# An attention and mixer kernel on one core: the first batch is normalised behind the product with the values, the second batch's x is turned by DMA, a third unit is loaded ahead of the branch

## The chip, the cores and the metric

The kernel runs on one core of a Trainium2 chip. The metric is the device time of one execution in microseconds. The core's engines are TensorE (PE in the profile, PEld for its weight loads), VectorE (DVE), ScalarE (ACT), GpSimd (POOL) and SyncE (SP), which issues nearly all DMA transfers.

## What is computed

Attention for 4 batches of 8 heads, 768 positions and head size 64, then a token mixer and a channel mixer, all in float32:

```python
def _attn_ref(q, k, v, n_global, n_local) -> np.ndarray:
    ...
    scores = scale * np.matmul(q, k.transpose(0, 1, 3, 2))
    ...
    keep = is_global | is_local
    ...
    scores = scores + bias[None, :, :, :]
    scores = np.where(keep, scores, -1000000000.0)
    scores = scores - np.max(scores, axis=-1, keepdims=True)
    a = np.exp(scores)
    a = a / (np.sum(a, axis=-1, keepdims=True) + 1e-09)
    return np.matmul(a, v).astype(np.float32)

def _moe_ref(x, w_tok1, w_tok2, w_ch1, w_ch2):
    xt = x.transpose(0, 2, 1)
    h = np.maximum(xt @ w_tok1, 0.0) @ w_tok2
    u = x + h.transpose(0, 2, 1)
    h2 = np.maximum(u @ w_ch1, 0.0) @ w_ch2
    return (u + h2).astype(np.float32)
```

Kept are 8 global columns and the 96 positions up to and with a query's own. Between the two, x is the attention's result with heads side by side: 768 positions by 512 channels per batch.

## The kernel before, in words

**Units.** A unit is two heads of one batch and 256 positions. There are 12 units per batch (`PER`), 48 in all. Because only near and global positions are kept, a unit's scores are two blocks of 128 query rows per head (the first positions, j = 0: 128 and 256 columns; later ones: 256 and 256). The two heads of a unit sit in the two halves of TensorE's rows or columns.

**A unit's steps** (`pair`, line 433): load; scale the queries (`q`, tile qs); scores (`S`, tile sp); maxima with the bias added on VectorE (`max`); exponentials with their sums on ScalarE (`exp`, tile pp or p; the statistics are in tile st); sums plus 1e-9 (`sum`) and inverses (`inv`); the scaling of the exponentials by the inverses (`norm`, line 486), always on GpSimd, one instruction per head and cut; the transposes (`T`, tile tp) and their copies back (`back`) or, from unit 20 on (`FAR`), the same by DMA through tile r; the product with the values (`V`, line 526, tile op), which gives x already transposed, channels by positions; and the copy of it to x on ScalarE (`put`, line 543). Units below 15 (`WIDE`) keep their exponentials in one wide tile pp.

**A batch's mixers.** `tokens` (line 592) needs x with positions in the partitions. The first batch turns x on TensorE by half batches (`nat_half`). The second batch (b < `NEAR` = 2) turns it on TensorE too (`nat`, line 602: six calls of four 128x128 transposes into tile xtp). The third and fourth have VectorE split x into 16-bit halves (`xs`, tile xr), eight DMA transposes on SP's queue (`xt`, tile xn), and a step that puts the halves together (`xw`). Then come high and low parts (ph, pl), products with the first token weights (`J`, tile pj), and with the second (`U`, tile pu). `channel` (line 778) is dense matmul work for the first three batches (tiles hp and acc), `blocks` (line 858) the same for the last in a form with fewer products; there the results are gathered in banks ga (512 columns for each of four channel blocks c) and ge (256 columns, one bank shared by blocks c and c + 1), added to x on VectorE (`total`) and stored.

**What sets the order.** `Plan` (line 117) is a list scheduler in Python that runs when the program is built. Every step has an engine (or a choice of engines, by cost), a cost, what it comes after, what it takes and gives (tiles, PSUM banks), and a rank. The planner steps through time and gives each free engine the ready step of least rank; a change between forms of matmul costs it 0.1 or 0.2. The ranks come from a table packed in text (`RANKS`, line 1117, read by `ranks`, line 1163, in eighths). Each engine then runs its instructions in that order and waits by semaphores.

**The start.** `Early` (line 72) stands ahead of a branch on the inputs `n_global` and `n_local`, whose words every engine first loads into registers (`program`, line 1346). It clears a tile, issues the DMAs for the queries and keys of units 0 and 1 (columns 128 to 640 of their tiles; the rest is issued behind the branch), builds positions and distances on GpSimd, and runs `WARM` = 7 matmuls on zeros:

```python
        for i in range(2):
            sp.dma_start(out=self.slots[i][:, 128:640], in_=pk[i, :, 128:640])
...
            for i in range(WARM):
                pe.matmul(out=wp, lhsT=warm[:, :P], rhs=warm, start=i == 0, stop=i == WARM - 1)
```

Units 2 to 11 are loaded whole behind the branch into tiles named unit; later units go through a ring of four tiles (`RING`), named e like the two early ones.

Of the kernel before, what the change touches and what calls it, by code (L numbers as in the profile page):

```python
# [9 lines left out]
F32 = mybir.dt.float32  # L10
# [5 lines left out]
BF16 = mybir.dt.bfloat16  # L16
AF = mybir.ActivationFunctionType
ALU = mybir.AluOpType
# [5 lines left out]
C = H * D  # L24
# [14 lines left out]
NEAR = 2  # L39
FIRST = 0  # L40
WARM = 7
# [30 lines left out]
class Early:  # L72


    def __init__(self, tc, pool, pk, nb):
# [3 lines left out]
        self.slots = [pool.tile([P, 1024], F32, tag=f"e{i}", name=f"e{i}") for i in range(3)]  # L79
# [5 lines left out]
        warm = t[:, 576:832].bitcast(BF16)  # L85
        dve.memset(warm, 0.0)
# [5 lines left out]
        for i in range(2):  # L92
            sp.dma_start(out=self.slots[i][:, 128:640], in_=pk[i, :, 128:640])
# [16 lines left out]

        with tc.tile_pool(name="warm", bufs=1, space=PSUM) as ps:
            wp = ps.tile([P, 512], F32, name="warm")
            for i in range(WARM):
                pe.matmul(out=wp, lhsT=warm[:, :P], rhs=warm, start=i == 0, stop=i == WARM - 1)


class Plan:
# [21 lines left out]
    def record(self):  # L139
# [21 lines left out]
        held_port, marks, sharing, slow = 0.0, [], None, 0.0  # L161
# [88 lines left out]
class Fast:  # L250
# [3 lines left out]
    def __init__(self, ctx, tc, early, pk, nb, w1, w2, wc1, wc2, out):  # L254
# [16 lines left out]
        self.ring = early.slots + [const.tile([P, 1024], F32, tag=f"r{i}", name=f"e{i}") for i in range(RING - 3)]  # L271
# [130 lines left out]
    def load(self, v, first=False):  # L402

        b, n, j = where(v)
        if v < 2:
            t = self.early.slots[v]
            k0, z = 640, 896
        else:
            t = self.wt.tile([P, 1024], F32, tag="w", name="unit") if b == 0 else self.ring[(v - PER) % RING]
            k0, z = (128, 896) if j == 0 else (0, 1024)  # L410
        if not first:
            self.sp.dma_start(out=t[:, k0:z], in_=self.pk[v, :, k0:z])
            if v < 2:
                return
# [3 lines left out]
    def scale(self, v, engine):  # L418

        n = where(v)[1]  # L420
        if v < 2:
            self.load(v, True)
# [10 lines left out]
    def pair(self, v):  # L433
# [5 lines left out]
        far = v >= FAR  # L439

# [35 lines left out]
        def sums():  # L476
            st = g["st"]
            if FIRST <= v < PER:
                pool.tensor_scalar(out=st[:, 8:12], in0=st[:, 4:8], scalar1=EPS, scalar2=0.0, op0=ALU.add, op1=ALU.add)
            else:  # L480
                dve.tensor_scalar(out=st[:, 8:12], in0=st[:, 4:8], scalar1=EPS, scalar2=None, op0=ALU.add)
# [44 lines left out]
        def values():  # L526
# [9 lines left out]

            blocks = ((0, 0, 256, 128), (1, 128, 128, 384), (2, 0, 128, 0))[:2 if j == 0 else 3]
# [12 lines left out]
        if v < 2:  # L550
            add(f"load{v}", "sp", 0.5, lambda: self.load(v), [], rank("load", v), lag=2.6)
        else:
            add(f"load{v}", "sp", (1.4 if j == 0 else 1.85) if v < PER else 0.6, lambda: self.load(v),
                [f"V{v - RING}"] if v >= PER + RING else [f"V{v - PER}"] if v in (PER, PER + 1) else [], rank("load", v),
                ["w"] if v < PER else [], lag=None if v < PER else 3.5)
        if v:
            add(f"q{v}", dict(dve=0.3, act=0.4, pool=0.48) if b == 0 else dict(pool=0.48), 0, lambda e: self.scale(v, e),
                [f"load{v}"] if v > 1 else [], r - 8, ["q"])
# [9 lines left out]
        add(f"sum{v}", *(("pool", 0.32) if FIRST <= v < PER else ("dve", 0.1)), sums, [f"exp{v}0", f"exp{v}1"], r - 12)  # L568
        add(f"inv{v}", "dve", 0.1, inverses, [f"sum{v}"], r - 12)
        for e in range(2):  # L570
            add(f"norm{v}{e}", dict(pool=0.95 if j else 0.83), 0, lambda en, e=e: norm(e, en), [f"inv{v}"], r, parts=2)
        if not far:
            add(f"T{v}", "pe", 0.88 if j else 0.66, transposes, [f"norm{v}0", f"norm{v}1"], r - 5,
# [4 lines left out]
            late, give = "back", wp + (["w"] if 1 < v < PER else [])  # L578
# [279 lines left out]
    def blocks(self, b):  # L858
# [173 lines left out]
        for c in range(4):  # L1032
            n = f"{b}_{f}_{c}"
            add(f"G{b}_{f - 1}_{c}", "pe", 1.04, lambda c=c: second(f - 1, c),
                [f"hl{b}{p}0{m}" for m in range(2)] + [f"low{5 + 2 * f}"] + [f"G{b}_{f}_{c - 1}e" if c else f"G{b}_{f - 2}_3"], k + 3 * c,
                (), ["hid", "hid"] if c == 3 else [])
            add(f"G{n}a", "pe", 0.7, lambda c=c: second(f, c, (0,)), [f"hl{b}{p}1{m}" for m in range(2)] + [f"low{7 + 2 * f}", f"G{b}_{f - 1}_{c}"],
                k + 3 * c + 1)
            add(f"G{n}e", "pe", 0.35, lambda c=c: second(f, c, (1,)), [f"G{n}a"], k + 3 * c + 2, (), ["hid", "hid"] if c == 3 else [])
            for m, x, cost, give in ((0, "a", 0.75, [("ga", b, c)]), (1, "e", 0.35, [("ge", b, c // 2)] if c % 2 else [])):  # L1040
                add(f"out{b}{c}{m}", "dve", cost, lambda c=c, m=m: total(c, m), [f"G{n}{x}"] + ([f"out{b}{c}0"] if m else []), r - 60, (), give)
                add(f"store{b}{c}{m}", "sp", 0.5, lambda c=c, m=m: store(c, m), [f"out{b}{c}{m}"], r - 60, lag=1.6)
# [37 lines left out]
BUSY = dict(dve=1.2, act=0.4, pool=3.0, sp=0.4)  # L1080


def rank(kind, *at):
# [34 lines left out]
    'c-jq>hhG#2;>D-;wllMpU0{JA)`-|n#2C8~xmY6_u_Tf+UPP=!&w^M2L8BOqX!K`@QDZD<L_Hz4Soy_H5yV(%A}GQxyF0tHGv|Ns-sgSad)t-KZ?5SP!'  # L1118
    'Ca&TT;VOz+|(cb!RT3}Q(umKj@)&}O5K88{AG~Le8vO-Cprm;MK&vCt}%=T*>werZOawD@t*<)KqWM*mJmOKuYytPdU=!b74@?#6`mf*&~P=!ejfNIe1'
    '{o8-Bc+4dFU)Mha90zBVzpX!<KR-L@C=}cIYdqI#adg;Bc^+O$}b~%#%zsPus!iOaT}kT);%=67f5k;2VIMse9s=xK4q5I*<9#U~~8o=8y!1ZzH!u60;'  # L1120
    '-va9v$+1U^_{z^&L{aHGZq^Su*wKQ!08kxGF}x$e|W=1;y4y&qV^&EOJUK{AN9lb;fhisA_OH}Do+t)C7$1J@7(@8p$$#MY`~*e7xc@fd%tXXx{wSXc-'
    'CL3byI6B=Eiy#ai$_K{(>`(QINn|VQwcq8bS@DEkgG7GziP$X%*Bu>{DI)H8R{)X*`0+3A}V~n@#LZ`Y)wII8g|HA$ha54|UnVjVQ6F;g?LB^P7A~xit'
# [288 lines left out]
```

## Time and profile before

| | us |
|---|---|
| median of 3 runs | 609.85 (609.1 to 610.99) |
| the profiled execution | 607.03 |
| its span, first to last instruction | 605.3 |
| TensorE busy | 589.9 (97%) |
| VectorE busy | 388.8 (64%) |
| ScalarE busy | 291.5 (48%) |
| GpSimd busy | 190.2 (31%) |
| DMA queue of SP, share of 16 engines' span | 37.9% |

The profile is of one execution. Busy time is the union of an engine's instructions; a matmul's end is modelled, so neighbours overlap in the rows and their distance is best read from start to start. A row of the timeline merges like instructions that follow one another (x8 is eight of them); what stands in brackets is the idle time ahead of it and what ended it. A float32 product shows as two instructions, a transpose as one. The line L63 is that of a helper that issues nearly everything, so operations are told apart by their tiles.

### The profile page before, as it was taken

The page shows a single profiled execution, that of the slowest core. Times are in us where ns is not written, and L with a number is a line of the kernel's source. Part 1 is how long each engine was busy: PE and PEld are TensorE (multiplying, and loading weights), DVE is VectorE, ACT ScalarE, POOL GpSimd, SP SyncE. Part 2 cuts the span into 40 slices and gives each one's busy share as a digit, 9 for nine tenths or more (in the row PEclk, how much of TensorE's full clock was granted, in tenths as well). Part 3 has the DMA queues.
Part 4 walks back from the last instruction along what each step waited for, and adds up shares of the span by engine and source line. Part 5 has one row for each costly group of instructions (what it writes and reads, how often), then busy time and mean ns, then how long its engine had stood idle before and what let it go on. Part 6 is the DMA issues. An engine that isn't in the chain of part 4 may idle for free. (4 is left out here: it accounts for less than half of the span.)

```text
span 605.3 us, 10574 instructions
## 1 busy us (share of the span) xinstructions
PE 589.9 (97%) x3735; PEld 536.9 (89%) x3735; DVE 388.8 (64%) x1007; ACT 291.5 (48%) x777; POOL 190.2 (31%) x303
## 2 busy tenths in 40 slices
PE   6999999999999999999999999999999999999996
PEld 4677799989989899889999999999889999999995
DVE  4989999896641377556854466656778478854223
ACT  5899979884331236452443224244553244332220
POOL 5788774644320035233321024343241020000000
PEclk9999999999999999999999999999999999999999
DMA  7971291632730012666937001766756000100003
GB/s 257 376 262 46 108 329 53 229 119 62 157 88 26 2 53 52 145 145 149 188 73 172 4 26 40 158 125 150 169 98 110 0 2 17 37 1 1 0 1 109
DMA packets 84172, 62.63 MB, mean 103 GB/s; under 512 B 69776, under 2 KB 74128, under 8 KB 84112
## 3 DMA queue, kind: packets, MB, share of 16 engines
q1 hardware_dynamic: 83968, 61.88, 37.9%
q8 instruction: 31, 0.51, 0.3%
q14 instruction: 29, 0.24, 0.1%
q10 hardware_dynamic: 144, 0.00, 0.0%
HBM read 38.80 MB, written 6.29 MB: 74 GB/s over the span
## 5 line engine op out<-in xcount | busy, mean ns | idle before, releaser
L63 PE MATMUL hp<-uh,wc 128*128 128x384 f32 x576 | 153.9, 337 | 0.0
L63 PE MATMUL acc<-hh,wc 128*128 128x384 f32 x576 | 148.7, 339 | 0.7 <-DVE hl L63 0.7
L63 PEld LDWEIGHTS acc<-hh,wc 128*128 128x128 f32 x576 | 102.8, 188 | 6.0 <-issue 3.8
L63 PEld LDWEIGHTS hp<-uh,wc 128*128 128x128 f32 x576 | 104.5, 188 | 3.6 <-issue 1.9
L63 POOL TENSOR_SCALAR p<-p,st 128x256 f32<-128x256 f32 (+1 forms) x132 | 77.7, 608 | 93.5 <-ACT p L63 49.3
L63 DVE COPY r<-p 128x1024 uint16<-128x1024 uint16 (+1 forms) x96 | 66.9, 717 | 54.4 <-DMA p<-r 33.6
L63 PE MATMUL acc<-hl,wc 128*128 128x384 f32 x288 | 96.7, 336 | 0.2 <-DVE hl L63 0.2
L63 PE MATMUL hp<-ul,wc 128*128 128x384 f32 x288 | 96.3, 334 | 0.0
L63 ACT ACTIVATE hh<-hp 128x384 fp32r<-128x384 f32 x72 | 35.1, 489 | 85.9 <-PE hp L63 58.6
L63 ACT ACTIVATE p<-p,st 128x256 f32<-128x256 f32 (+1 forms) x132 | 63.6, 484 | 14.2 <-DVE st L63 14.2
L63 DVE SCALAR_TENSOR_TENSOR hl<-hp,hh 128x384 fp32r<-128x384 f32 x72 | 39.3, 550 | 41.0 <-ACT hh L63 36.3
L63 PEld LDWEIGHTS acc<-hl,wc 128*128 128x128 f32 x288 | 54.0, 188 | 0.7 <-DVE hl L63 0.7
L63 PEld LDWEIGHTS hp<-ul,wc 128*128 128x128 f32 x288 | 54.1, 188 | 0.1
L63 POOL TENSOR_TENSOR ul<-x,uh 128x384 fp32r<-128x384 f32 x19 | 21.3, 1125 | 97.2 <-ACT uh L63 93.2
L63 POOL TENSOR_SCALAR qs<-e,sc 128x256 f32<-128x256 f32 x36 | 22.1, 617 | 57.3 <-DMA e<-pk 51.8
L63 PE MATMUL sp<-e,qs 64*128 64x256 f32 (+1 forms) x304 | 38.0, 384 | 1.0 <-DVE few L63 0.9
L63 ACT COPY r<-p 128x1024 uint16<-128x1024 uint16 (+1 forms) x16 | 20.8, 1302 | 36.0 <-DMA p<-r 28.5
L63 POOL TENSOR_SCALAR pp<-pp,st 128x256 f32<-128x256 f32 (+1 forms) x60 | 33.1, 569 | 4.5 <-DVE st L63 4.2
L63 PEld LDWEIGHTS sp<-e,qs 64*128 64x128 f32 x304 | 26.4, 194 | 8.6 <-issue 3.6
L63 PE MATMUL ga<-hh,wc 128*128 128x512 f32 x96 | 30.2, 395 | 0.0
L63 ACT ACTIVATE pp<-pp,st 128x256 f32<-128x256 f32 (+1 forms) x60 | 28.5, 481 | 3.0 <-DVE st L63 2.9
L63 PE MATMUL op<-r,e 128*64 128x128 f32 (+1 forms) x304 | 27.6, 318 | 0.7 <-DVE st L63 0.4
(146 smaller groups left out, 1096.8 us busy)
## 6 DMA issues: line engine op xcount, KB each, us to landing
w<-wc SPq DMA_DIRECT2D x24, 512.0 KB, 6.1
e<-pk SPq DMA_DIRECT2D x24, 512.0 KB, 4.3
e<-pk SPq DMA_DIRECT2D x12, 384.0 KB, 3.6
out<-o SPq DMA_DIRECT2D x24, 192.0 KB, 1.9
unit<-pk SPq DMA_DIRECT2D x8, 512.0 KB, 7.9
w<-w SPq DMA_DIRECT2D x6, 512.0 KB, 9.5
out<-x SPq DMA_DIRECT2D x8, 192.0 KB, 1.9
p<-r SPq DMA_TRANSPOSE x56, 3.4
```

The lines of the kernel that those rows point to most:

```text
L63: ins = getattr(self.engine, name)(*args, **kw)
```

## The change

- **Third unit.** The ring's fourth tile is made early. Keys and queries of unit 2 are loaded into it ahead of the branch, as a third DMA on SP; the rest of it follows behind the branch with that of units 0 and 1. Unit 15, which uses this ring tile next, now waits for unit 2's product.
- **Warm matmuls.** Four instead of seven, and behind the register loads, ahead of the branch.
- **First batch (`fold`).** No scaling by the inverses ahead of the transposes, which now wait for the exponentials alone. The product with the values is preceded by four matmuls that write the inverses of each query column, broadcast over 64 rows, to columns 256 to 512 of the same bank. ScalarE copies that part to x (`pi`), VectorE multiplies the product with it (`put`). Sums may go to GpSimd or VectorE.
- **Second batch.** `NEAR` = 1: x is turned like that of the third and fourth.
- **Last products.** In even channel blocks of the last stage the 256-column part (ge) goes ahead of the 512-column part (ga); in odd ones it stays behind.
- **Planner.** It takes the first 3.4 us of TensorE for slow, the engines are free a little later (`BUSY`), and all ranks are replaced by a new table in halves.

The diff, cut to its core (the new table of ranks is left out):

```diff
-NEAR = 2
+NEAR = 1
-WARM = 7
+WARM = 4
...
-        for i in range(2):
-            sp.dma_start(out=self.slots[i][:, 128:640], in_=pk[i, :, 128:640])
+        for i, x, k in ((0, 0, 128), (1, 1, 128), (2, 3, 0)):
+            sp.dma_start(out=self.slots[x][:, k:640], in_=pk[i, :, k:640])
...
+    def warm(self, tc):
         with tc.tile_pool(name="warm", bufs=1, space=PSUM) as ps:
...
-        held_port, marks, sharing, slow = 0.0, [], None, 0.0
+        held_port, marks, sharing, slow = 0.0, [], None, CRAWL
...
-        if v < 2:
-            t = self.early.slots[v]
-            k0, z = 640, 896
+        if v < 3:
+            t = self.early.slots[(0, 1, 3)[v]]
+            k0, z = 640, 896 if v < 2 else 1024
...
+        fold = b == 0
...
+            for i, e in ((i, e) for i in range(2 if fold else 0) for e in range(2)):
+                k = 8 + 2 * e + i
+                self.pe.matmul(out=op[64 * e:64 * e + 64, 256 + P * i:256 + P * i + P], lhsT=g["st"][:, k:k + 1].broadcast_to([P, 64]),
+                               rhs=self.ident, start=True, stop=True)
...
-        def put():
+        def put(step=0):
             for m, o, c, w in (((0, 0, 0, 256),), ((0, 256, 0, 128), (1, 0, 128, 128)), ((1, 128, 0, 256),))[j]:
-                act.copy(out=self.x[b, n, m][:, o:o + w], in_=g["op"][:, c:c + w])
+                x, y = self.x[b, n, m][:, o:o + w], g["op"]
+                if step == 1:
+                    dve.tensor_tensor(out=x, in0=y[:, c:c + w], in1=x, op=ALU.mult)
+                else:
+                    act.copy(out=x, in_=y[:, c + 256 * fold:c + 256 * fold + w])
...
-        for e in range(2):
+        for e in range(0 if fold else 2):
             add(f"norm{v}{e}", dict(pool=0.95 if j else 0.83), 0, lambda en, e=e: norm(e, en), [f"inv{v}"], r, parts=2)
         if not far:
-            add(f"T{v}", "pe", 0.88 if j else 0.66, transposes, [f"norm{v}0", f"norm{v}1"], r - 5,
+            add(f"T{v}", "pe", 0.88 if j else 0.66, transposes, [f"{'exp' if fold else 'norm'}{v}{e}" for e in range(2)], r - 5,
...
-        add(f"V{v}", "pe", 0.86 if j else 0.65, values, ([f"load{v}"] if v < 2 else []) + [f"{late}{x}{e}" for x in twins for e in range(2)] + ([f"V{v - (4 if b else 2)}"] if twins and j else []) or [f"V{v - 1}"],
+        add(f"V{v}", "pe", (0.86 if j else 0.65) + 0.25 * fold, values, ([f"load{v}"] if v < 3 else []) + ([f"inv{v}"] if fold else []) + [f"{late}{x}{e}" for x in twins for e in range(2)] + ([f"V{v - (4 if b else 2)}"] if twins and j else []) or [f"V{v - 1}"],
-        add(f"put{v}", "act", 0.34 if j == 1 else 0.28, put, [f"V{v}"], r - 15, (), [("op", v)])
+        if fold:
+            add(f"pi{v}", "act", 0.34 if j == 1 else 0.28, put, [f"V{v}"], r - 15)
+            add(f"put{v}", "dve", 0.45 if j == 1 else 0.35, lambda: put(1), [f"pi{v}"], r - 15, (), [("op", v)])
+        else:
+            add(f"put{v}", "act", 0.34 if j == 1 else 0.28, put, [f"V{v}"], r - 15, (), [("op", v)])
...
+            order = (("e", 0.35), ("a", 0.7)) if c % 2 == 0 else (("a", 0.7), ("e", 0.35))
+            for i, (x, cost) in enumerate(order):
+                add(f"G{n}{x}", "pe", cost, lambda c=c, x=x: second(f, c, (0 if x == "a" else 1,)),
...
-BUSY = dict(dve=1.2, act=0.4, pool=3.0, sp=0.4)
+BUSY = dict(dve=1.8, act=0.8, pool=3.0, sp=1.0)
...
-    return [x / 8.0 for x in struct.unpack(f"<{len(data) // 2}h", data)]
+    return [x / 2.0 for x in struct.unpack(f"<{len(data) // 2}h", data)]
...
     _, (g_lo, g_hi, l_lo, l_hi) = nc.values_load_multi_w_load_instructions(nb)
+    early.warm(tc)
```

## Rows read from the trace of the kernel before

**Rows 1.** The page: busy times (shares of the span), and TensorE in 40 slices.

```profile
PE 589.9 (97%) x3735; PEld 536.9 (89%) x3735; DVE 388.8 (64%) x1007; ACT 291.5 (48%) x777; POOL 190.2 (31%) x303
PE   6999999999999999999999999999999999999996
```

**Rows 2.** Table by stretches: stretch and length, busy us per engine, PEclk, DMA, GB/s.

```profile
10.86:15.62 4.76, 4.76 (x20) 3.61 (x21) 2.83 (x12) 2.84 (x10) 2.97 (x9) 1.00 1.02 417
15.62:45.00 29.38, 26.94 (x239) 20.79 (x239) 25.87 (x92) 27.19 (x87) 22.60 (x41) 1.00 0.86 316
45.00:81.00 36.00, 34.96 (x281) 28.58 (x281) 33.76 (x96) 35.08 (x105) 30.64 (x45) 1.00 0.31 113
```

**Rows 3.** Timeline of TensorE from the start: start us, length, instructions, idle before.

```profile
1.20 3.17 PE L63 MATMUL warm<-e 128*128 128x512 bf16 x7 [1.20 <-DVE e L63]
5.25 2.93 PE L63 MATMUL sp<-e,qs 64*128 64x128 f32 x16 [0.89 <-DVE few L63]
10.86 2.08 PE L63 MATMUL sp<-unit,qs 64*128 64x256 f32 x8 [2.67 <-DVE qs L63]
12.87 2.82 PE L63 MATMUL tp<-ident,pp 128*128 128x128 f32 x12
15.62 1.42 PE L63 MATMUL sp<-unit,qs 64*128 64x256 f32 x8
16.97 1.52 PE L63 MATMUL op<-pp,e 128*64 128x256 f32 x16
18.43 1.13 PE L63 MATMUL sp<-unit,qs 64*128 64x256 f32 x8
```

**Rows 4.** Timeline: SP's issues for units 0 to 2, and unit 2's scaling.

```profile
0.75 0.89 SPq L63 DMA_DIRECT2D e<-pk  x2
...
4.68 0.81 SPq L63 DMA_DIRECT2D e<-pk  x2
...
5.53 0.43 SPq L63 DMA_DIRECT2D unit<-pk  x1
...
10.45 0.35 DVE L63 TENSOR_SCALAR qs<-unit,sc 128x256 f32<-128x256 f32 x1 [0.82 <-DMA unit<-pk]
```

**Rows 5.** Timeline of TensorE: transposes of the second batch's x, first twelve.

```profile
195.06 1.47 PE L63 MATMUL xtp<-ident,x 128*128 128x128 f32 x12
...
196.29 0.60 PE L63 MATMUL acc<-hh,wc 128*128 128x384 f32 x2
```

**Rows 6.** Groups on GpSimd, 0 to 80 us: busy us, mean ns, idle before.

```profile
L63 POOL TENSOR_SCALAR pp<-pp,st 128x256 f32<-128x256 f32 x46 | 25.9, 575 | 3.8 <-DVE st L63 3.6
...
L63 POOL TENSOR_SCALAR pp<-pp,st 128x128 f32<-128x128 f32 x14 | 7.7, 549 | 0.7 <-DVE st L63 0.6
```

**Rows 7.** Timeline of TensorE: the value products of two later units.

```profile
27.30 1.96 PE L63 MATMUL op<-pp,unit 128*64 128x256 f32 x24
29.18 1.13 PE L63 MATMUL sp<-unit,qs 64*128 64x256 f32 x8
```

**Rows 8.** Groups on VectorE, whole span: the nearest product out of PSUM.

```profile
L63 DVE TENSOR_TENSOR x<-ge,x 128x256 f32<-128x256 f32 x4 | 1.7, 419 | 1.2 <-PE ge L63 1.2
```

**Rows 9.** Tiles xr and xn, later batches: duration ns min/median/max, then landing.

```profile
L63 DVE COPY xr<-x x16: 532/554/1653, 273.5 to 463.9; 128x768 uint16<-128x768 uint16 x16
L63 SPq DMA_TRANSPOSE xn<-xr x16: 1212/1234/1572, 275.0 to 466.7; - x16
...
L63 DVE COPY xw<-xn x8: 741/748/761, 323.8 to 473.8; 128x1024 uint16<-128x1024 uint16 x8
...
DMA to landing us min/median/max: 2.8/3.0/6.2
```

**Rows 10.** Timeline near the end: the weight load that waits for VectorE.

```profile
599.06 0.30 PEld L63 LDWEIGHTS ge<-hh,wc 128*128 128x128 f32 x2 [0.25 <-DVE x L63]
```

**Rows 11.** Timeline: second batch's last copy to x, first token product.

```profile
192.96 0.38 ACT L63 COPY x<-op 128x256 f32<-128x256 f32 x1 [0.54 <-PE op L63]
...
199.36 0.39 PE L63 MATMUL pj<-ph,w1h 128*128 128x512 f32 x1
```

More of the change, by code (lines that the diff above doesn't have):

```diff
@@ L77, in __init__ @@
         pe, dve, act, gps, sp = [InOrder(tc, e) for e in (nc.tensor, nc.vector, nc.scalar, nc.gpsimd, nc.sync)]
-        self.slots = [pool.tile([P, 1024], F32, tag=f"e{i}", name=f"e{i}") for i in range(3)]
+        self.slots = [pool.tile([P, 1024], F32, tag=f"e{i}", name=f"e{i}") for i in range(RING)]
         self.ni = pool.tile([P, 4], I32, tag="ni", name="ni")
@@ L84, in __init__ @@
         t = self.slots[2]
-        warm = t[:, 576:832].bitcast(BF16)
-        dve.memset(warm, 0.0)
+        self.zeros = t[:, 576:832].bitcast(BF16)
+        dve.memset(self.zeros, 0.0)
         self.one = t[:, 832:836]
@@ L113, in __init__ @@
             for i in range(WARM):
-                pe.matmul(out=wp, lhsT=warm[:, :P], rhs=warm, start=i == 0, stop=i == WARM - 1)
+                tc.nc.tensor.matmul(out=wp, lhsT=self.zeros[:, :P], rhs=self.zeros, start=i == 0, stop=i == WARM - 1)
 class Plan:
@@ L269, in __init__ @@
         const = self.const = pool("const", 1)
-        self.ring = early.slots + [const.tile([P, 1024], F32, tag=f"r{i}", name=f"e{i}") for i in range(RING - 3)]
+        self.ring = early.slots
         self.wt = pool("wt", 2 * NF)
@@ L474, in exps, with sums @@
                                bias=g["st"][:, k:k + 1], accum_out=g["st"][:, 4 + k:5 + k])
-        def sums():
+        def sums(engine):
             st = g["st"]
[L478 to L481, printed above, removed]
+            engine.tensor_scalar(out=st[:, 8:12], in0=st[:, 4:8], scalar1=EPS, scalar2=0.0, op0=ALU.add, op1=ALU.add)
         def inverses():
@@ L557, in pair @@
             add(f"q{v}", dict(dve=0.3, act=0.4, pool=0.48) if b == 0 else dict(pool=0.48), 0, lambda e: self.scale(v, e),
[L558 removed]
+                [f"load{v}"] if v > 2 else [], r - 8, ["q"])
         wp = ["w"] if wide else ["p", "p"]
@@ L577, in pair @@
                     r - 10, (), [("tp", v, e)])
-            late, give = "back", wp + (["w"] if 1 < v < PER else [])
+            late, give = "back", wp + (["w"] if 2 < v < PER else [])
         else:
@@ L1034, in blocks @@
             add(f"G{b}_{f - 1}_{c}", "pe", 1.04, lambda c=c: second(f - 1, c),
-                [f"hl{b}{p}0{m}" for m in range(2)] + [f"low{5 + 2 * f}"] + [f"G{b}_{f}_{c - 1}e" if c else f"G{b}_{f - 2}_3"], k + 3 * c,
+                [f"hl{b}{p}0{m}" for m in range(2)] + [f"low{5 + 2 * f}"] + [f"G{b}_{f}_{c - 1}{'ea'[c % 2]}" if c else f"G{b}_{f - 2}_3"], k + 3 * c,
                 (), ["hid", "hid"] if c == 3 else [])
-            add(f"G{n}a", "pe", 0.7, lambda c=c: second(f, c, (0,)), [f"hl{b}{p}1{m}" for m in range(2)] + [f"low{7 + 2 * f}", f"G{b}_{f - 1}_{c}"],
-                k + 3 * c + 1)
-            add(f"G{n}e", "pe", 0.35, lambda c=c: second(f, c, (1,)), [f"G{n}a"], k + 3 * c + 2, (), ["hid", "hid"] if c == 3 else [])
+            order = (("e", 0.35), ("a", 0.7)) if c % 2 == 0 else (("a", 0.7), ("e", 0.35))
+            for i, (x, cost) in enumerate(order):
+                add(f"G{n}{x}", "pe", cost, lambda c=c, x=x: second(f, c, (0 if x == "a" else 1,)),
+                    [f"G{n}{order[0][0]}"] if i else [f"hl{b}{p}1{m}" for m in range(2)] + [f"low{7 + 2 * f}", f"G{b}_{f - 1}_{c}"],
+                    k + 3 * c + 1 + i, (), ["hid", "hid"] if c == 3 and i else [])
             for m, x, cost, give in ((0, "a", 0.75, [("ga", b, c)]), (1, "e", 0.35, [("ge", b, c // 2)] if c % 2 else [])):
-                add(f"out{b}{c}{m}", "dve", cost, lambda c=c, m=m: total(c, m), [f"G{n}{x}"] + ([f"out{b}{c}0"] if m else []), r - 60, (), give)
-                add(f"store{b}{c}{m}", "sp", 0.5, lambda c=c, m=m: store(c, m), [f"out{b}{c}{m}"], r - 60, lag=1.6)
+                add(f"out{b}{c}{m}", "dve", cost, lambda c=c, m=m: total(c, m), [f"G{n}{x}"] + ([f"out{b}{c}{1 - m}"] if m == c % 2 else []), r - 60, (), give)
+                add(f"store{b}{c}{m}", "sp", 0.5, lambda c=c, m=m: store(c, m), [f"out{b}{c}{x}" for x in range(m + 1)], r - 60, lag=1.6)
     def run(self):
```

95 lines of the change are left out of this document (48 added, 47 removed).

## The prediction
> **What bounds the kernel now.** I read the page's shares first. TensorE is busy for 589.9 of 605.3 us and its row of slices reads 9 everywhere except in the first and the last slice [rows 1]. So the bound is TensorE's work plus its few idle stretches, and an edit counts only by the matmul time it adds or takes away, or by an idle or slow stretch of TensorE that it closes. The table by stretches comes next: from 15.62 to 45 us TensorE idles 29.38 - 26.94 = 2.4 us and from 45 to 81 us 1.0 us, together 3.5, while ScalarE works 27.19 of 29.38 and 35.08 of 36, VectorE 25.87 and 33.76, GpSimd 22.60 and 30.64 [rows 2]. In this stage (first batch) all engines are nearly full; after it TensorE alone is. Then TensorE's own timeline from the start. The scores of units 0 and 1 begin at 5.25, unit 2's at 10.86, after 2.67 us of idleness that ended with the scaled queries qs [rows 3]. Why so late: SP issues two loads ahead of the branch (0.75 to 1.64), gets past the branch at 4.68, issues unit 2 only at 5.53, and VectorE, which scales it at 10.45, had waited for that DMA [rows 4].
>
> **The clock at the start.** The granted clock column reads 1.00 from 10.86 to 15.62 [rows 2], but the matmuls say otherwise: the eight instructions of unit 2's scores take 2.08 us at 10.86 and the same eight 1.13 at 18.43, and twelve transposes take 12.87 to 15.62 = 2.75 us [rows 3] where twelve later ones take 195.06 to 196.29 = 1.23 [rows 5]. So until about 15.6 us the array is at the lower of its two levels, 1.2 GHz, and from then at 2.4. Ahead of the rise TensorE had worked without a gap since 10.86; the seven warm matmuls and the first scores, with gaps of 0.89 and 2.67 us between, had not brought it.
>
> **The change part by part.**
>
> *Third unit ahead of the branch.* Unit 2's keys and queries come behind units 0 and 1 on SP's queue, into a slot of their own, so its scores can follow unit 1's at 8.2 us: the 2.67 us go. On SP's queue the third issue costs some 0.4 us (two took 0.89 [rows 4]), so all that SP issues behind the branch, from the first two values halves to unit 3 and the weights, comes 0.4 us later; one values load more (unit 2's) stands there too. Their next user is unit 3's scores, at 15.62 now, which leaves cover; without it those scores would come 0.8 us later. Term: **-2.7**. With no idle stretch in the way the clock should rise earlier. If it rises at the end of unit 2's scores, the twelve transposes save 2.75 - 1.23 = 1.5 us; if also during the first scores, up to some 4 us; if it still rises at 15.6, the 2.67 us won are worked at half speed and 1.3 of them are lost again. I take **-1.5**, between +1.3 and -4, by the transposes, the work that stands right behind.
>
> *Warm matmuls.* Four instead of seven, behind the register loads. Seven take 3.17 us, so four take 1.8 [rows 3]. SP's stretch from its last issue at 1.64 to 4.68 bounds the register loads and branch at 3.0 us [rows 4]. Starting with them, TensorE would be through by about 3.5 and warm until 5.3, and unit 0's scores start at 5.25 anyway, so between 0 and +0.2; I take 0. Cover gone (loads slower), each microsecond is one of delay.
>
> *Normalisation behind the product.* The first batch loses its GpSimd scalings between exponential and transpose. Up to 80 us GpSimd has 46 of 575 ns and 14 of 549 ns on wide tiles [rows 6], four for each of the fifteen units that use such tiles; twelve of these are the first batch, so 48 go, about 27 us. They lie on GpSimd, not on TensorE, so directly they give nothing; but each unit's way from exponential to transpose is 4 x 0.57 = 2.3 us shorter. In their place TensorE gets four matmuls per unit, each a column of inverses broadcast against the identity, 128 columns, one per head and cut. No such matmul is in the trace; the nearest are the value products of the same output shape. Two units with two blocks take 16.97 to 18.43 = 1.46 us, 0.73 each [rows 3], two with three blocks 27.30 to 29.18 = 1.88, 0.94 each [rows 7]: one 128-column block for both heads costs 0.21. Two blocks per unit and twelve units: **+5.0**, all on the path, since TensorE is the bound. The planner's own cost is 0.25 per unit, 3.0 in all; I take the rows, and keep 3.0 as the lower end and, should the broadcast weights load slower, 6.5 as the upper. ScalarE copies as many columns as before. VectorE gets the multiplication, nearest row x<-ge at 0.42 us for 256 columns out of PSUM [rows 8]: some 12 x 0.45 = 5.4 us, against 5.8 us of idleness in rows 2, and GpSimd's freed 27 us can take subtractions and scalings off it. The product now also waits for the inverses, and the output bank is held by two steps instead of one.
>
> *Waits of TensorE from 15.6 to 81.* 3.5 us [rows 2]. The softmax chain is shorter, GpSimd is free, but VectorE has more to do. Between none left (-3.5) and 3 us more, I take half of them gone: **-1.7**. The new table of ranks reorders everything here and shows in no row; these bounds are to hold it.
>
> *Second batch's x turned by DMA.* TensorE loses 24 transposes (six calls of four). Twelve took 1.23 us [rows 5]: **-2.5**. In their place VectorE splits (0.55 us, eight), SP's queue carries eight DMA transposes (1.23 us of issue, 3.0 to land), and VectorE puts halves together (0.75 us, six), as the later batches do [rows 9]; 15 us or so of VectorE and SP in a stretch where TensorE has a channel stage to work on. The casts and subtractions behind stay. Cover gone: rival D.
>
> *Order of the last matmuls.* The last product into ge of an odd column block waits 0.25 us for VectorE's read of the even one, at 599.06 [rows 10] and once more, 4.3 us earlier in the same pattern. With ge first in even blocks the read falls under the 512-column products: **-0.5**, at worst 0. The last block keeps its order, so the end stays.
>
> Sum: -2.7 - 1.5 + 5.0 - 1.7 - 2.5 - 0.5 = **-3.9 us**. The profiled execution took 607.03 us, 605.3 of span and 1.7 around it, and would come to 603.1; it lies 2.8 us below the median of the runs shown, 609.85, which by the same difference gives 605.95, **606.0 us**. What a measurement of this kernel can tell from no change is 0.3%, 1.8 us.
>
> **Rivals.**
>
> *B, VectorE becomes the bound (slower).* Place: 15.6 to 81 us. It works 59.6 of 65.4 us there [rows 2]. If it keeps its share of idleness (it waits on the others in turn) and gets 5.4 us more with nothing taken off, the stage takes 65.4 x 65.0 / 59.6 = 71.3 us, 5.9 more, and the start's gain becomes waits for the multiplied x. Left are +5.9 - 2.5 - 0.5 = +2.9: **612.8**. It decides while GpSimd takes less than about 3 us off VectorE, for each of them gives back 1.1. For it: the shares above. Against: GpSimd freed by 27 us, and the start's work 2.7 us earlier.
>
> *C, the start gives little.* Clock rise unchanged, waits in the stage down by only 1.2: -2.7 + 1.3 + 5.0 - 1.2 - 2.5 - 0.5 = -0.6: **609.3**. This is also what comes out if the change doesn't do what it says, unit 2 landing early but being scaled late. For it: the row that shows the rise tells only what went before it. Against: GpSimd idles early, and can scale.
>
> *D, the turned x comes late.* After the second batch's last copy (192.96, 0.38 us) the first product with the token weights starts at 199.36 [rows 11], 6.0 us later, filled with other matmuls. The way by DMA takes 0.55 + 4 x 1.23 + 3.0 + 0.75 = 9.2 us for a half of four tiles. If nothing fills it, 3.2 us are lost: **609.2**. Against: the first half's tiles are ready sooner, only the second half hangs on the last copy, and TensorE waits nearly nowhere in later batches, which turn x this way. The Trainium skill, VectorE: DVE Perf Modes, "Rules for kernel authors", speaks against this part: a 128x128 transpose belongs on TensorE where the result may go to PSUM, and on the DMA crossbar only otherwise. The rows agree that one transpose is far shorter there, 0.10 against 1.23 us of issue alone. By that rule the sum would be better without this part's -2.5, or it comes to this rival; the rule does not ask which engine is full.
>
> *E, all ends good.* Broadcasts at 3.0, the clock up during the first scores, no waits left: -2.7 - 4.0 + 3.0 - 3.5 - 2.5 - 0.5 = -10.2: **599.7**.
>
> **Chances and numbers.** The forecast 0.55, as TensorE's own terms are read from rows and its start is plainly idle; E 0.10, C 0.17, D 0.05, B 0.13. Faster by over 0.3%: forecast and E, 0.65. Within 0.3%: C and D, 0.22. Slower: B, 0.13. The range runs from 601.0, which leaves out E's far end, to 611.5, which holds C and D and the forecast with costlier broadcasts, and leaves out most of B. The forecast's own range is 603 to 608.
>
> **What would show it.** Unit 2's scores right behind unit 1's at some 8.2 us, and the doubled durations gone before 12 us. 48 (or 96, as float32 instructions come in pairs) new TensorE rows from the statistics and the identity, whose stretch per unit is 0.42 us; 0.25 or less would set that term too high. No first-batch scaling of exponentials on GpSimd. The rows xtp halved, 24 DMA transposes xn instead of 16, no TensorE wait near 200 us. No wait for ge at the end. Idle TensorE between 15 and 81 us under 3.5. Wrong if TensorE's idleness there grows by more than the start gains, above all with VectorE named as the releaser, or if the clock rises no earlier.

## The result, and the profile after

The changed kernel takes **601.31 us** (median of six runs, 600.73 to 602.05), the kernel before on the same chip 609.57 (six runs, 608.05 to 610.99): ratio 0.9865, 95% interval 0.9848 to 0.9882, or **8.3 us less**. The forecast said faster, by 3.9, to 606.0, with its own range from 603 to 608; the result lies 0.3 us inside the lower end of the whole range, 601.0. A second set gave 601.12 against 608.26, ratio 0.9885 (0.986 to 0.9911). The profiled executions differ less, 607.03 and 601.20, because the one of before lies below all six runs above: two more took 609.99 and 608.21.

The page's shares and slices of the changed kernel: TensorE still bounds it, and GpSimd has lost 12.6 us.

```profile
PE 587.3 (98%) x3804; PEld 537.7 (90%) x3804; DVE 392.8 (66%) x1026; ACT 297.3 (50%) x778; POOL 177.6 (30%) x265
PE   7999999999999999999999999999999999999996
```

The table by stretches, to be held against [rows 2]. TensorE's idleness between 15.62 and 81 us falls from 3.5 to 0.9 us; VectorE fills up (28.09 of 29.38), GpSimd empties (12.59 for 22.60).

```profile
10.86:15.62 4.76, 4.76 (x40) 3.60 (x41) 4.76 (x23) 4.30 (x18) 0.94 (x3) 1.00 1.04 412
15.62:45.00 29.38, 28.48 (x286) 23.21 (x284) 28.09 (x98) 28.12 (x89) 12.59 (x17) 1.00 0.92 354
45.00:81.00 36.00, 36.00 (x317) 30.50 (x314) 32.72 (x109) 33.16 (x99) 23.67 (x33) 1.00 0.26 89
```

TensorE's timeline from the start, against [rows 3]. The scores of units 0, 1 and 2 are one row without a pause, but they begin at 6.10, 0.85 us later than before.

```profile
1.20 1.89 PE L115 MATMUL warm<-e 128*128 128x512 bf16 x4 [1.20 <-DVE e L63]
6.10 4.64 PE L63 MATMUL sp<-e,qs 64*128 64x128 f32 x24 [3.02 <-DVE e L63]
10.68 1.26 PE L63 MATMUL tp<-ident,pp 128*128 128x128 f32 x6
11.87 1.14 PE L63 MATMUL sp<-unit,qs 64*128 64x256 f32 x8
12.93 0.88 PE L63 MATMUL tp<-ident,pp 128*128 128x128 f32 x6
...
14.80 0.66 PE L63 MATMUL op<-ident,st 128*64 128x128 f32 x8
15.29 0.82 PE L63 MATMUL op<-pp,e 128*64 128x256 f32 x8
15.94 0.61 PE L63 MATMUL op<-ident,st 128*64 128x128 f32 x8
16.37 0.82 PE L63 MATMUL op<-pp,e 128*64 128x256 f32 x8
```

The broadcasts (op from ident and st) take 0.49 and 0.43 us a unit, start to start. SP's queue, against [rows 4], has a third issue ahead of the branch, and its next one at 5.71 instead of 4.68. The first scaling of queries on VectorE, which waits for its load in both kernels, starts at 4.90 instead of 4.38. With the third load taken out again (below) the scores start at 5.22, so the third load is what makes the start late; through which step all of the 0.85 comes, no row tells.

```profile
0.75 1.36 SPq L63 DMA_DIRECT2D e<-pk  x3
5.71 0.33 SPq L63 DMA_DIRECT2D unit<-pk  x1
```

TensorE's list of waits is short (engine, tile, what it waited for; us in all, times, longest): two at the start, one among the first batch's transposes (at 34.4) and three in the later mixers. Its weight loads, which [rows 10] showed waiting for VectorE ahead of ge, stand without a wait from 586 us on.

```profile
PE sp L63 <- DVE e L63: 3.0, 1, 3.0
PE warm L115 <- DVE e L63: 1.2, 1, 1.2
PE acc L63 <- DVE st L63: 0.9, 2, 0.5
PE tp L63 <- DVE pp L63: 0.8, 1, 0.8
PE hp L63 <- DVE hl L63: 0.2, 1, 0.2
```

The list of before has three entries that lie between 15.62 and 81 us and that are gone here. The first stands at 21.39, and the profile shows nothing that ended it.

```profile
PE sp L63 <- issue: 1.2, 1, 1.2
...
PE op L63 <- ACT pp L63: 1.0, 3, 0.4
...
PE xtp L63 <- ACT x L63: 0.8, 1, 0.8
```

**Two stages.** The first product of the channel stage (tile hp) is a good milestone: in either order the same TensorE work stands ahead of it, but for the broadcasts, three warm-up products fewer and one more unit's scores (1.06 us) in the changed kernel. Read from the timelines:

| kernel | hp starts | from there to TensorE's end | idle in that part |
|---|---|---|---|
| before, three profiles | 80.90, 80.87, 79.98 | 518.78, 521.09, 520.18 | 1.47, 2.67, 1.95 |
| changed, two profiles | 80.12, 79.84 | 513.44, 513.08 | 1.05, 1.04 |

So up to the milestone the change wins 80.58 - 79.98 = 0.6 and 1.06 of work done, 1.7 us; behind it 520.0 - 513.3 = 6.8, of which 1.06 is that work, so 5.7. The forecast had 0.9 and 3.0. These are few profiles, though. Four of the variants below (without the third unit, without the fold, with 7 and with 10 warm-up products) have the changed kernel's work and order behind hp, and there they take 514.15, 515.57, 513.55 and 514.87. The six together have a mean of 514.1, and the 5.7 becomes 4.8.

### The profile page after: what moved, and what is told of

It is laid out like the page before. It is cut to its first block, busy times and chain, and to the rows that moved or that the text cites. A ratio compares the mean times of both kernels' runs of the same rounds, so it can differ in the third digit from the quotient of the medians.

```text
span 599.1 us, 10678 instructions
## 1 busy us (share of the span) xinstructions
PE 587.3 (98%) x3804; PEld 537.7 (90%) x3804; DVE 392.8 (66%) x1026; ACT 297.3 (50%) x778; POOL 177.6 (30%) x265
## 4 chain that ended last, share of the span: by engine, by line
PE 56%; DMA 3%; DVE 2%; issue 0%; ACT 0%; SPq 0%; DVEq 0%
PE acc L63 16%; PE hp L63 13%; PE ga L63 6%; PE X L63 4%; PE op L63 3%; PE pj L63 3%; PE pu L63 3%; PE ge L63 3%; PE sp L63 2%; PE W L63 2%; DMA p<-r 2%; PE Y L63 1%; DMA xn<-xr 1%; DVE r L63 1%; DVE o L63 1%; DVE p L63 0%
## 5 line engine op out<-in xcount | busy, mean ns | idle before, releaser
L63 DVE COPY r<-p 128x1024 uint16<-128x1024 uint16 (+1 forms) x89 | 63.7, 732 | 40.3 <-DMA p<-r 24.9
L63 POOL TENSOR_TENSOR ul<-x,uh 128x384 fp32r<-128x384 f32 x23 | 25.4, 1109 | 94.3 <-ACT uh L63 92.4
L63 ACT COPY r<-p 128x1024 uint16<-128x1024 uint16 (+1 forms) x23 | 29.1, 1285 | 29.1 <-DMA p<-r 17.5
L63 PE MATMUL sp<-e,qs 64*128 64x256 f32 (+1 forms) x312 | 39.3, 389 | 3.0 <-DVE e L63 3.0
L63 PEld LDWEIGHTS sp<-e,qs 64*128 64x128 f32 x312 | 27.8, 197 | 10.9 <-issue 8.4
L63 ACT COPY x<-op 128x256 f32<-128x256 f32 (+1 forms) x64 | 18.9, 322 | 25.6 <-PE op L63 25.4
L63 DVE CUSTOM_DVE_ANT_0 p<-sp,be 128x256 f32<-128x256 f32 x48 | 20.0, 416 | 12.2 <-PE sp L63 10.8
```

The lines of the kernel that those rows point to most:

```text
L63: ins = getattr(self.engine, name)(*args, **kw)
```

## Experiments

All ratios are against the kernel before, run on the same chip in the same set. Differences in us are between medians of a set; where the ratio gives another difference by 0.4 us or more, it stands beside. In each variant but the one of before with more warm-up products, the order is written out as a list, and where a part was taken out or put in, the list was mended. The profile of a variant is one of its executions, and not always a usual one.

**The changed kernel with its order written out**, a second sample of it.

> The changed kernel, with every engine's order of work written out as a list in place of the ranks; the instructions and their order are the changed kernel's own. Account theory and order theory alike: 601.3, within 0.5 of the changed kernel's median, so that the variants beside it can be set against it. If it comes out more than 1 us from that, the variants may only be compared with one another. Its profile is a second execution of the changed kernel: if the start is what makes executions differ, the granted clock should rise at another time than the 11.8 us of the first profile.

601.12 us (600.04 to 601.74), ratio 0.9885 (0.986 to 0.9911). Its profile repeats the first, the scores of units 0 to 2 at the low level again. The variants below are set against 601.12.

**Without the third unit ahead.**

```diff
-        if v < 3:
-            t = self.early.slots[(0, 1, 3)[v]]
...
+        if v < 2:
+            t = self.early.slots[v]
...
```

> The changed kernel and its order, but unit 2 is loaded whole behind the branch. Account theory (what TensorE waits for at the start is lost for good): 2.7 for the wait, 1.4 for the clock's later rise, less 0.85 because the branch is left earlier with two loads ahead of it: 3.2 us slower than the changed kernel. Rival (the start is caught up later, since the units behind it wait for other things): 0 to 1 us slower.

606.63, ratio 0.9978 (0.9962 to 0.9993): 5.5 us above the changed kernel, more than either theory. Its third unit is scored at 12.68, after 4.53 us of waiting for queries that ScalarE scaled only when their load had come, and still at the low level. hp starts at 85.03, 5.1 later: what is lost at the start is not caught up. The rival falls.

```profile
12.68 2.08 PE L63 MATMUL sp<-unit,qs 64*128 64x256 f32 x8 [4.53 <-ACT qs L63]
```

**Without the folded normalisation.**

```diff
-        fold = b == 0
+        fold, FIRST_ = False, b == 0
...
-        for e in range(0 if fold else 2):
+        for e in range(2):
...
```

> The changed kernel with the first batch normalised by GpSimd ahead of its transposes again, no broadcasts on TensorE; over the first 85 us of the plan the order is mended where work would otherwise stand behind a later normalisation, elsewhere it is the changed kernel's. Account theory (the fold costs 5.0 of broadcasts and gives back 2.6 of waits): 2.4 us faster than the changed kernel. Rival (the shorter chain is what lets the early order run without waits, so that it is worth more than its broadcasts): 2 to 7 us slower than the changed kernel, with the loss in waits for normalised p and the probabilities' copies before 81 us.

607.77, ratio 0.9987 (0.9965 to 1.0009): 6.6 us above the changed kernel (6.2 by the ratios) although 5.7 us of broadcasts are gone. The account theory falls, and the time is what the rival said. TensorE's waits in this kernel:

```profile
PE tp L63 <- POOL pp L63: 2.7, 3, 1.9
...
PE op L63 <- DVE pp L63: 1.3, 2, 0.8
```

The transposes wait for GpSimd's normalised p, which the changed kernel does not have to wait for. Only part of the 6.6 us can be read, as this execution (604.95) was 2.8 us under its own median. Its hp starts at 82.31, 2.3 later: TensorE idles 3.8 us more ahead of it, the rows of op are 1.9 and those of the scores 1.8 us longer, the broadcasts' 5.7 are gone. The scores are longer because a unit's eight still take 2.08 us at 14.90, the low level, where the changed kernel has 1.14 at 11.87.

**Without x by DMA.**

```diff
-NEAR = 1
+NEAR = 2
```

> The changed kernel with the second batch's x turned by TensorE again (six groups of four transposes, no DMA transposes of x, no packing and unpacking copies); from 125 to 230 us of the plan the order is mended where it would stall. Account theory: the transposes' 2.5 us of TensorE come back, 2.5 us slower than the changed kernel. Rival D (x turned by DMA comes late and its copies load VectorE): the same or up to 0.7 us faster than the changed kernel.

604.82, ratio 0.9947 (0.993 to 0.9964): 3.7 us above the changed kernel. hp starts at 79.91, so all of it lies behind. Summed by tile over that part, from one group's start to the next, the transposes xtp add 2.5 us and TensorE's idleness 1.1 (2.11 for 1.04), in these waits above all:

```profile
PE hp L63 <- DVE hl L63: 0.7, 1, 0.7
...
PE op L63 <- DVE r L63: 0.5, 1, 0.5
PE op L63 <- ACT p L63: 0.2, 1, 0.2
```

Only the first of them, at 195.6, stands where the turned x is used. The 0.5 is at 294, and TensorE's idleness behind hp is 1.04 to 2.45 us in the six profiles with the changed kernel's work there. Against their mean of 514.1 this kernel's 516.95 is 2.8 longer. So the account theory's 2.5 stands and rival D falls; that the part is worth more than its transposes is not shown, as the two ratios' intervals leave 1.2 to 6.3 us.

**Without the exchange of the last products** (the lines of the diff that make `order` go back).

> The changed kernel with the last products and output sums of the last channel in the order of the kernel before. Account theory: the last sum waits again for the bank of the second products, 0.5 us slower than the changed kernel (601.7). Rival (the output store behind it hides it): the same within 0.2.

602.25, ratio 0.9891 (0.9867 to 0.9914) against 0.9885 for the changed kernel: 0.4 us by the ratios, 1.1 by the medians of two sets on two chips, not told apart from nothing.

**The third unit alone, in the old order.**

```diff
-        for i in range(2):
-            sp.dma_start(out=self.slots[i][:, 128:640], in_=pk[i, :, 128:640])
+        for i, x, k in ((0, 0, 128), (1, 1, 128), (2, 3, 0)):
+            sp.dma_start(out=self.slots[x][:, k:640], in_=pk[i, :, k:640])
...
```

> The kernel before and its order, with the third unit's k and q loaded ahead of the branch; units 2 and 4 change places in the first steps, so that unit 2, not unit 4, is scored third. Account theory: the wait of 2.7 less 0.85 for the later branch, and 1.4 for the clock's earlier rise: 3.2 us faster than before. Rival (given back: the transposes of the first units now wait for normalised p, since the order behind is the old one): 0 to 1 us faster.

611.39, ratio 1.0045 (1.003 to 1.0061), **2.8 us slower** than before. Both theories fall as to the time; of the rival's mechanism there is more than it asked. The timeline shows where the 2.67 us went: into new waits of the transposes for GpSimd. And the low level lasts longer: a unit's scores take 2.08 us at 16.16 and the value products behind them are slow too, where before has the scores at 1.13 from 18.43 and sixteen value products in 1.52 [rows 3].

```profile
5.84 4.55 PE L63 MATMUL sp<-e,qs 64*128 64x128 f32 x24 [1.47 <-DVE e L63]
11.55 1.22 PE L63 MATMUL tp<-ident,pp 128*128 128x128 f32 x6 [1.16 <-POOL pp L63]
14.45 1.78 PE L63 MATMUL tp<-ident,pp 128*128 128x128 f32 x6 [1.68 <-POOL pp L63]
16.16 2.08 PE L63 MATMUL sp<-unit,qs 64*128 64x256 f32 x8
18.17 2.39 PE L63 MATMUL op<-pp,e 128*64 128x256 f32 x12
```

**The folded normalisation alone, in the old order** (the diff's lines in `pair` on fold, norm, pi and put).

> The kernel before and its order, with the first batch normalised behind the product with the values (48 broadcasts more on TensorE, 24 normalisations less on GpSimd, 24 multiplications on VectorE). Account theory: broadcasts 5.0 less the waits for normalised p that go, 2 to 2.6: 2.4 to 3 us slower than before. Rival (the order was made for the long chain, nothing is gained): 5 us slower. Rival (the chain was what held the start): 0 to 1 us slower.

611.98, ratio 1.0047 (1.0028 to 1.0065), 3.4 slower (2.9 by the ratio): nearest to the account theory, under the first rival's 5. In its profile hp starts at 85.63, 5.0 later, for 5.7 of broadcasts: TensorE idles 1.6 us less ahead of it, and its scores take 1.3 more.

**Three parts together, in the old order** (third unit, fold, last products).

> The kernel before and its order with three of the four parts: third unit ahead, normalisation behind the product, last products exchanged; x of the second batch is still turned by TensorE. Account theory: -3.2 + 2.6 - 0.5: 1.1 us faster than before, so that the order and x by DMA hold the remaining 7. Rival (the parts help each other: with the third unit ahead and no normalisation to wait for, the start runs through): 4 to 5 us faster than before.

611.76, ratio 1.007 (1.0044 to 1.0095), 3.2 slower than before (4.3 by the ratio); both theories fall. hp starts at 84.83, although the first scores ran at the high level and the transposes began at 8.33:

```profile
5.95 2.44 PE L63 MATMUL sp<-e,qs 64*128 64x128 f32 x24 [1.62 <-DVE bo L63]
8.33 1.52 PE L63 MATMUL tp<-ident,pp 128*128 128x128 f32 x7
...
12.29 1.13 PE L63 MATMUL sp<-unit,qs 64*128 64x256 f32 x8 [0.97 <-POOL qs L63]
13.36 0.66 PE L63 MATMUL op<-ident,st 128*64 128x128 f32 x8
16.16 0.87 PE L63 MATMUL op<-pp,e 128*64 128x256 f32 x8 [2.14 <-ACT pp L63]
```

The product of unit 0 now stands waiting for ScalarE's copy of the transposed p. Between unit 0's transposes and this product the old order has unit 1's transposes and one unit's scores; the changed order has a second unit's scores there as well, and shows no wait.

**The new order alone**, with none of the four parts.

```diff
-NEAR = 1
+NEAR = 2
...
-        if v < 3:
...
+        if v < 2:
...
-        fold = b == 0
+        fold, FIRST_ = False, b == 0
...
```

> The changed kernel's order of work, from the changed kernel's table, without any of the four parts: unit 2 loaded whole behind the branch, the first batch normalised by GpSimd ahead of the transposes, the second batch's x turned by TensorE, the last products as before; over the first 230 us of the plan the order is mended where work would stall. Theory 'the order is worth something by itself' (the parts lose 3 us in the old order, the order gains 10 with or without them): about 600. Theory 'the order is only good for the parts' (what the three parts cost when each is taken out of the changed kernel adds up, 5.5 + 6.6 + 3.7): 617.

612.8, ratio 1.0071 (1.0046 to 1.0096), 4.4 slower; the second theory is nearer, but nothing adds up. hp starts at 87.11, with two units' scores (2.1 us) more ahead of it than in before, and the start shows the units' scores late again:

```profile
5.22 2.93 PE L63 MATMUL sp<-e,qs 64*128 64x128 f32 x16 [2.13 <-DVE few L63]
9.03 2.08 PE L63 MATMUL sp<-unit,qs 64*128 64x256 f32 x8 [0.88 <-POOL qs L63]
12.84 2.08 PE L63 MATMUL sp<-unit,qs 64*128 64x256 f32 x8 [1.74 <-ACT qs L63]
```

With three parts (all but x by DMA) and the order, this makes a table of four corners, each against before in its own set:

| | without the three parts | with them |
|---|---|---|
| old order | 0 | +3.2 (three parts) |
| new order | +4.4 (order alone) | -3.4 (without x by DMA) |

Parts and order each lose by themselves; together they win 3.4, which is 11.0 us under the sum of the two losses (11.8 by the ratios). The row of the new order also has the four warm-up products in place of seven, whose number is worth nothing measurable below. And what the third unit, the fold and x by DMA cost when each is taken out of the changed kernel adds up to 15.8, twice what the change wins.

**x by DMA alone, in the old order.**

```diff
-NEAR = 2
+NEAR = 1
```

> The kernel before and its order, with the second batch's x turned by DMA instead of by TensorE; the packing copies stand where the attention output that they read comes, the unpacking copies behind the last unit's maxima, and from 188 to 230 us of the plan the order is mended where it would stall. Account theory: 2.5 us of transposes go, 2.5 us faster than before. Rival D (the turned x comes late: the last unit's output is ready shortly before the products with it, and packing, DMA, unpacking and splitting now stand between them): 1 to 5 us slower than before, with waits of the products pj for the copies around 190 to 210 us.

609.71, ratio 1.0012 (0.999 to 1.0033): no difference, so the account theory falls. Rival D does not stand either: there is no wait of pj, and no loss clear of noise. Of the transposes' 2.4 us nothing is left: behind hp TensorE idles 5.20 us, against 1.5 to 2.7 in before, above all at 123.0 and at 213.0:

```profile
PE sp L63 <- POOL qs L63: 1.4, 1, 1.4
...
PE pu L63 <- DVE pl L63: 0.9, 1, 0.9
```

**Warm-up products.** Three runs on the clock at the start.

```diff
-WARM = 4
+WARM = 7
```

> The changed kernel with 7 warm-up products in place of 4, nothing else. Theory of the early clock (the scores of units 0 to 2 run at the low level, 0.19 us a product, as TensorE stood for 3.0 us before them; in the profile of the three parts in the old order, with 7 warm-up products, they took 0.10): the stretch from the first score to the first transpose falls from 4.6 to 2.4 us, and the kernel becomes up to 2.2 us faster. Rival (the exponentials of unit 0 are not there earlier; TensorE waits for them instead): the same within 0.5, with a new wait ahead of the first transposes.

602.57, ratio 0.9898 (0.9873 to 0.9924); hp at 79.31, and no wait ahead of the first transposes. The stretch from the first score to the first transpose fell only from 4.6 to 4.0 us, so this profile decides neither theory; no time was won.

```profile
5.82 4.04 PE L63 MATMUL sp<-e,qs 64*128 64x128 f32 x24 [1.45 <-DVE e L63]
```

And with 10:

> The changed kernel with 10 warm-up products in place of 4, so that TensorE works up to 5.7 us. Theory: the scores of units 0 to 2 take 2.4 in place of 4.6 us, and since nothing waits there the kernel gains 1 to 2 us (600). Rival (the exponentials set the start): tp waits, the first channel's products start within 0.5 us of 79.9, the time is the same within 0.5.

602.93, ratio 0.9902 (0.9886 to 0.9918), so nothing won and at most a little lost; hp at 79.0. The scores of units 0 to 2 now run at the high level, and 2.2 us are won there; the next units' scores then wait for GpSimd's scaled queries, as the rival says of waits, though on another tile:

```profile
5.75 2.44 PE L63 MATMUL sp<-e,qs 64*128 64x128 f32 x24 [0.76 <-DVE e L63]
8.13 1.24 PE L63 MATMUL tp<-ident,pp 128*128 128x128 f32 x6
9.86 1.13 PE L63 MATMUL sp<-unit,qs 64*128 64x256 f32 x8 [0.49 <-POOL qs L63]
10.92 1.19 PE L63 MATMUL tp<-ident,pp 128*128 128x128 f32 x6
13.17 1.14 PE L63 MATMUL sp<-unit,qs 64*128 64x256 f32 x8 [1.06 <-POOL qs L63]
```

The kernel before with 9 in place of 7:

> The kernel before with 9 warm-up products in place of 7, so that TensorE works up to the first scores at 5.25 us. Theory (the clock's rise changes the time and the long pause ahead of the third unit does not bring it down again): the first scores run at the high level, the first channel's products start 2 us earlier, 606.5. Rival (the scores of units 0 and 1 only end earlier and TensorE waits longer for the third unit; what follows is at the low level again, or the waits take the rest): the same within 1 us.

609.48, ratio 1.0007 (0.9982 to 1.0032), hp at 80.41: the first scores ran at the high level (1.73 us for 16), then came 3.24 us of waiting, then the low level again. The rival stands.

**The kernel before, twice more.**

> The kernel before itself. 609.6, within 0.5. Its profile is a second execution. Theory of the early clock (the profiled execution of before, 2.5 us under its own median, was one in which the granted clock happened to rise early): this profile's execution shows the rise later than 15.4 us into the span, and a span nearer 607.5. Rival (the difference is a drift of all stages alike): the rise is at 15.4 again, and the times of the groups differ by a few tenths of a per cent throughout.

> The kernel before a third time, for its profile alone. If the 2.3 us by which the second profile was longer behind 81 us is chance from execution to execution: the first channel's products at 80.9 or 78.7, and from there to the end between 518.8 and 521.1.

608.67 (12 runs, 607.6 to 610.41; ratio 1.0005, 0.9989 to 1.0021) and one run of 608.21. The theory of a lucky early rise falls: the profiled execution of before had the late rise (hp at 80.90) and was short behind hp. The second profile is 2.3 us longer there: 1.2 in waits of 0.1 to 0.7 us at places that change from profile to profile, the rest inside rows. The third had hp at 79.98, between the two values expected, and 520.18 behind it, within them: what is chance behind hp spans 2.3 us in three executions. It had its first scores at the high level, and still the third unit's late:

```profile
5.25 1.58 PE L63 MATMUL sp<-e,qs 64*128 64x128 f32 x16 [0.88 <-DVE few L63]
10.85 1.54 PE L63 MATMUL sp<-unit,qs 64*128 64x256 f32 x8 [4.01 <-DVE qs L63]
12.31 2.75 PE L63 MATMUL tp<-ident,pp 128*128 128x128 f32 x12
```

## Why the prediction had the sign but half the size

The time fell within the range, 0.3 us from its end and outside the forecast's own 603 to 608; the sum was too small by more than half. Rival E's 599.7 is the nearest number, but by luck: the broadcasts took 5.7 us and not 3.0, the first scores ran at the low level, and waits were left. By its steps:

- **Third unit, -2.7.** The wait is gone, as said, but the third load costs more than the 0.4 us counted for SP: the scores start 0.85 later, so 1.8 is left. One label was wrong: the unit scored at 10.86 in before is unit 4, the third in the planner's order; its queries' wait is the same thing.
- **Clock, -1.5.** The doubled durations end before 12 us, as said. The rows of scores and transposes ahead of hp take 2.2 us less for the same work than in the first profile of before, 1.4 less than in the mean of the three. A still earlier rise wins nothing: forced with 10 warm-up products it moved hp by 0.8 to 1.1 us and no measured time, and in before by nothing measurable. What the changed kernel would lose with a late rise, no run tells.
- **Warm matmuls, 0.** They start at 1.20 as before and end at 3.09, not by 3.5; TensorE then idles 3.02 us, and the scores behind run at the low level, not warm until 5.3. Seven and ten of them won no time, so the term stands.
- **Broadcasts, +5.0.** The broadcasts take 5.71 us ahead of hp, 0.48 a unit where 0.42 was counted. The value products take 13.50 for 14.18 in before, so that both together come to +5.03. The planner's 3.0 was rightly left at the end of the range.
- **Waits from 15.6 to 81, -1.7.** They fell by 2.6, and 1.25 of that is the gap at 21.39 that the profile puts down to nothing. VectorE's 16 multiplications (5.3 us, 349 ns each) came as forecast, and rival B did not happen.
- Together to hp: -0.9 forecast, -1.7 measured.
- **x by DMA, -2.5.** Taking it out of the changed kernel costs 3.7 by the medians and 2.8 by the profiles behind hp; the transposes are 2.5 of either, as counted, and the rest is not told from chance. Rival D did not happen in the new order: of the four DMA transposes that it hung on the last copy only one is issued behind it (186.71, then 187.71), and the first product of that half stands at 197.48. In the old order the gain was all given back. D's 0.10 against 1.23 us also set one 128x128 transpose against an issue that turns three blocks' worth in 16-bit halves. The Trainium skill, VectorE: DVE Perf Modes, "Rules for kernel authors", would have kept the 128x128 transposes on TensorE. The 3.7 us speak against it where TensorE is the bound and the order leaves time for the longer way; the old order, where nothing was gained, does not.
- **Last products, -0.5.** No ge wait is left; its worth is not resolved.
- **The step that failed** is the one on waits: "I take half of them gone", for 15.6 to 81 us alone, with the new ranks to stay within those bounds, and no term for waits behind 81 but ge's. Summed by tile behind hp, changed against the mean of before: xtp -2.4, idle -1.0, op -1.5 and hp -0.8 (the same products, op in 18 groups both times, in less time inside the groups, so it is likely that short waits stood there), the scores, of which one unit's moved, -0.7, the rest -0.4. With all six profiles that share the changed kernel's work behind hp it is idle -0.6, op -1.3, hp -0.8, and acc +0.5. So some 2 to 3 us of waits went there that the forecast had at nothing; the list of waits shows 1.0 of them at most, and the cause of the rest, inside rows, stays open.
- The base was another part of the miss. The sum was worked out on one execution of 607.03, whose waits behind 81 us were the smallest of three (1.47, 2.67 and 1.95 us): it showed less to win than a usual execution has. From the three profiles' mean (608.4) to the changed kernel's two (601.1) is 7.3 us. Of these 1.7 lie ahead of hp, 2.5 are the transposes and some 0.4 the last products; 2.7 are left for waits behind hp, or 1.9 by the six profiles. How that divides between order and chance, no run here tells.

Besides, the sum took the parts as independent of the order and of each other, and the four corners show that they are not. The third unit alone runs into GpSimd's normalisation; the fold removes that, and alone it costs more than it gives back. That both need an order that fills the time between transpose and product is read from the 2.14 us wait of the three parts together; no run tests it by itself. One caution: the old and new lists were mended by the planner's rule for these mixed kernels, not searched again, so a better order for each may exist.

## What to carry to other kernels

Where the order of work is fixed by a table, an edit and its order are one change: price the order by what stands late next after each removed wait, and do not expect the parts alone to win: here three of them lost together and one won nothing. Before summing small terms on one profile, look at how far that execution stands from its own median, and at whether its waits are the usual ones. A wait taken off the start is only worth what the next engine in the chain can follow.

## What was not expected of the hardware

The same instructions start at either clock level from execution to execution. In before, the 16 first scores at 5.25 us, after 0.9 us of idleness and seven warm-up products, took 2.93 and 2.94 us in two profiles and 1.58 in the third, and 1.58 in the kernel with x by DMA alone, whose start is the same. There the high level held over a pause of 2.91 us; in the third profile of before, after one of 4.01 us, the twelve transposes took 2.75 again:

```profile
5.23 1.58 PE L63 MATMUL sp<-e,qs 64*128 64x128 f32 x16 [0.86 <-DVE few L63]
9.72 1.13 PE L63 MATMUL sp<-unit,qs 64*128 64x256 f32 x8 [2.91 <-DVE qs L63]
10.78 0.88 PE L63 MATMUL tp<-ident,pp 128*128 128x128 f32 x6
```

In that execution hp started at 78.67, 2.2 us earlier than in the first profile of before; at 607.62 it was the shortest of its kernel's twelve runs, whose median did not differ from before. The granted clock column read 1.00 over those 2.93 us of the first profile too, so here the durations tell the level. Runs of before spread over 6 us in a set of 27 (605.65 to 611.69) and over 2.9 in a set of six, those of the changed kernel over 1.3 and 1.7 in two sets of six; so few runs do not show whether the spread differs.
